# Sliding attention beside an FFT convolution on one core: offset pairs in partition groups, x by DMA transpose, 128-column FFT stationaries, two plane products, negative powers from conjugates

## The chip, the cores and the metric

The kernel runs on one core of one Trainium2 chip. The metric is the device time of one execution in microseconds (us), as a median over several runs. Engines are named as in the profile: PE is TensorE (matmuls), PEld its weight load, DVE is VectorE, ACT is ScalarE, POOL is GpSimd, and SP is SyncE, which here does nothing but issue DMA transfers. "L404" is a line of the kernel file.

## The reference, cut to what matters

Two independent halves are computed from different inputs and joined along the last axis.

```python
# A: 32 heads of 20 channels, 2048 positions; each position sees itself and
#    7 earlier ones, two apart
qkv    = x @ wqkv
logits = einsum("bhsd,bhswd->bhsw", q, k[pos - 2*w]) * scale     # w = 0..7, masked where < 0
o      = einsum("bhsw,bhswd->bhsd", softmax(logits), v[pos - 2*w]) @ wo
# B: a state-space convolution of 640 channels and 192 states, by FFT of length 4096
dt = exp(log_dt);  P = exp(dt * (A_re + 1j*A_im) * l)            # l = 0..2047
K  = einsum("dn,dnl,dn->dl", C, P, dt*B).real                    # the filter taps
y  = irfft(rfft(u) * rfft(K))[:2048] + u * Dskip
out = concat([A, B], axis=-1)                                    # 1 x 2048 x 1280, bf16
```

## The kernel before

Half B works in five chunks of 128 channels. For a chunk, DVE builds two tables of complex powers, X (20 coarse powers) and Y (33 fine powers), from a few generators that wait in DRAM. PE multiplies them into the filter taps ("kgen"). Then come two FFT steps (`f1`, `f2`), a complex product of spectra, and the first inverse step `ia`, whose result Z goes to DRAM for the second inverse step. Blocks of attention are put between the chunks. These are the parts that the argument below touches; cuts are marked with `...`.

```python
def table_tiles(pools):                       # two X tables, one Y table
    tp = pools["tab"]
    return (tp.tile([128, 20, 2, CW], bf16, name="Xtab", tag="Xtab", bufs=2), ...  # Xg
            tp.tile([128, NB, 2, CW], bf16, name="Ytab", tag="Ytab"))

def kgen(tc, pools, X, Y, Kd):
    ...                                       # matmuls of 20 x 33 into PSUM
        nc.scalar.copy(out=Kd[:, :, t0:t0 + nt], in_=ps[:].rearrange("p t b -> p b t"))

def f2_prod(tc, pools, C, A1, Yf):
    ...
            nc.scalar.copy(out=S[:, 2 * h:2 * h + 2], in_=ps[:])          # 512 elements in a row

def ia(tc, pools, C, Yf, Z):
    ...                                       # runs of 4 elements, 64 bytes apart
        nc.scalar.copy(out=Z[:, :, :, 4 * jq:4 * jq + 4].rearrange("p l r (j d) -> p (l r) j d", d=2),
                       in_=ps[:].rearrange("p j l r d -> p (l r) j d"))

    def make(c):                              # load generators, build tables, make the taps
            ...
            nc.sync.dma_start(out=XT[:, 0], in_=Gd[c, :, 12])
            nc.sync.dma_start(out=Xg[:], in_=Gd[c, :, 0:6])
            for k in range(6):
                nc.sync.dma_start(out=Y[:, 2 ** k], in_=Gd[c, :, 6 + k])
        X, Y = tables(tc, pools, tt[c])
        ...
        kgen(tc, pools, X, Y, Kds[c])
```

The softmax here doesn't subtract the row's maximum and nothing guards it: scores larger than these inputs give would overflow.

## Time and profile before

The time before is 511.86 us (median of 3 runs, 509.21 to 513.9).

| | before |
|---|---|
| span of the profiled run, mean granted clock | 511.0 us, 0.876 |
| busy: PE / DVE / ACT / POOL | 368.9 / 360.2 / 269.0 / 104.8 us |
| SP: DMA transfers issued, time spent issuing | 184, 93.7 us |
| DMA packets | 83,596 |

The first lines are from the page of the kernel before: its span, the busy time of every engine with share and number of instructions, and the shares of the chain of waits that ended last, by engine.

```profile
span 511.0 us, 13799 instructions
PE 368.9 (72%) x5943; PEld 243.2 (48%) x5943; DVE 360.2 (70%) x528; ACT 269.0 (53%) x517; POOL 104.8 (21%) x192
PE 36%; DVE 28%; DMA 15%; ACT 12%; issue 6%; SPq 1%; POOL 0%; ACTq 0%; POOLq 0%; DVEq 0%
```

No engine is full and the chain changes hands between PE and DVE. A table of windows tells more than an average. Its columns are the stretch, its length, and then for PE, PEld, DVE, ACT and POOL the busy time and the number of instructions, at last the granted clock, the DMA share and GB/s.

```profile
150.00:200.00 50.00, 30.35 (x765) 22.74 (x766) 46.51 (x68) 17.86 (x32) 2.36 (x9) 0.73 0.55 160
250.00:300.00 50.00, 39.84 (x703) 29.20 (x693) 48.05 (x62) 28.74 (x56) 11.66 (x22) 0.92 0.53 129
300.00:350.00 50.00, 42.56 (x837) 30.00 (x836) 44.13 (x62) 25.17 (x47) 11.64 (x22) 0.91 0.19 50
```

DVE is busy 44 to 48 of 50 us here: in the middle of the kernel DVE sets the pace. The ACT copies out of PSUM are these two groups, split by shape. The columns are line, engine, operation, out<-in, shapes, count, then busy us and mean ns of one, then the idle time before them and what ended it.

```profile
L365 ACT CAST Z<-ps_ia 128x512 bf16<-128x512 f32 x24 | 14.6, 676 | 9.1 <-PE ps_ia L364 9.0
L288 ACT CAST Kd<-ps_k 128x363 bf16<-128x363 f32 x10 | 4.6, 463 | 31.0 <-PE ps_k L286 31.0
```

The Z copies of 128x512 took 0.676 us on average, with their output in runs of 4 elements at 64-byte steps (alone in p1_probe, below, such runs took 585 ns, as contiguous output did). The prediction leaned on that 0.676.

### The profile page before, as it was taken

Reading aid. Unit: us, or ns where it says so; the run is one execution under the profiler, and the core shown is the slowest. Engines: PE = TensorE matmul, PEld = TensorE weight load, DVE = VectorE, ACT = ScalarE, POOL = GpSimd, SP = SyncE. Lnnn points to the kernel's source line nnn. Section 1 sums busy time; section 2 is a strip of 40 time slices with the busy share of each in tenths; the row PEclk is TensorE's granted clock in tenths of the full one; section 3 lists DMA queues with packets and bytes.
Section 4 is the critical chain, followed back from the end, with each engine's and each line's share of the span. In section 5 each row is a group of like instructions: output and inputs, shape, how many; then the busy total and the mean of one; then the engine's idle time right before and its main releaser. Section 6 shows DMA issues by size and latency. Waiting matters only on the chain.

```text
span 511.0 us, 13799 instructions
## 1 busy us (share of the span) xinstructions
PE 368.9 (72%) x5943; PEld 243.2 (48%) x5943; DVE 360.2 (70%) x528; ACT 269.0 (53%) x517; POOL 104.8 (21%) x192
## 2 busy tenths in 40 slices
PE   2868799874752778798879868699495855987720
PEld 1543334631220566666656755476263533765520
DVE  0326899651899997999999977998948753636012
ACT  4466895758682435656355723467224522656610
POOL 7605500055000001000170001070001341143012
PEclk9999999997795788799988978999779969997955
DMA  7964946359669352220236432043609597622262
GB/s 197 267 145 129 225 123 208 104 168 255 215 211 314 118 110 66 60 115 3 61 66 204 114 66 57 1 132 83 139 13 347 146 299 192 197 48 39 91 187 41
DMA packets 83596, 70.99 MB, mean 139 GB/s; under 512 B 51744, under 2 KB 75104, under 8 KB 81872
## 3 DMA queue, kind: packets, MB, share of 16 engines
q1 hardware_dynamic: 75456, 55.90, 39.0%
q0 software_dynamic: 6368, 13.16, 10.7%
q10 hardware_dynamic: 1712, 1.07, 0.8%
q8 instruction: 46, 0.75, 0.7%
q14 instruction: 14, 0.11, 0.1%
HBM read 42.86 MB, written 24.13 MB: 131 GB/s over the span
## 4 chain that ended last, share of the span: by engine, by line
PE 36%; DVE 28%; DMA 15%; ACT 12%; issue 6%; SPq 1%; POOL 0%; ACTq 0%; POOLq 0%; DVEq 0%
PE ps_o L493 6%; DVE krtmp L226 4%; PE ps_k L286 4%; PE ps_k L281 4%; PE ps_op L508 3%; DMA Gdram<-cs 3%; DMA xn<-in_A_x_dram 3%; PE ps_s L310 3%; ACT S L344 3%; DMA zq<-Zdram_61 3%; DMA out_dram<-ud 3%; DVE Ytab L225 3%; DVE prod L468 2%; PE ps_p L428 2%; DMA uq<-Udram 2%
## 5 line engine op out<-in xcount | busy, mean ns | idle before, releaser
L468 DVE TENSOR_TENSOR prod<-qb,kb 128x2048 bf16<-128x2048 bf16 x40 | 48.7, 1233 | 2.0 <-PE ps_l L471 2.0
L502 POOL DMA_DIRECT2D oT<-vb x64 | 36.7, 581 | 48.1 <-ACT vb L494 43.8
L429 ACT CAST st<-ps_p 128x512 bf16<-128x512 f32 x60 | 34.1, 581 | 12.6 <-PE ps_p L428 12.3
L428 PE MATMUL ps_p<-xT,w_324 128*128 128x512 bf16 x100 | 28.0, 439 | 13.7 <-ACT st L429 13.6
L364 PE MATMUL ps_ia<-cEA,Yf 128*32 128x256 bf16 x640 | 29.1, 333 | 7.9 <-DVE Yf L350 6.7
L494 ACT CAST vb<-ps_o 128x512 bf16<-128x512 f32 x20 | 13.1, 653 | 37.2 <-PE ps_o L493 37.1
L286 PE MATMUL ps_k<-Ytab,Xtab 64*20 64x33 bf16 x1280 | 25.8, 243 | 9.3 <-issue 9.2
L342 PEld LDWEIGHTS <-cT 128*64 128x64 bf16 x640 | 23.3, 114 | 18.9 <-issue 18.3
L288 ACT CAST Kd<-ps_k 128x363 bf16<-128x363 f32 (+1 forms) x15 | 6.8, 453 | 47.2 <-PE ps_k L286 47.2
L471 PE MATMUL ps_l<-prod,cGs 128*32 128x512 bf16 x160 | 18.3, 435 | 17.6 <-DVE prod L468 17.4
L225 DVE TENSOR_TENSOR Ytab<-Ytab 128x2688 bf16<-128x2688 bf16 (+3 forms) x25 | 30.8, 1234 | 0.0
L364 PEld LDWEIGHTS <-Yf 128*32 128x32 bf16 x640 | 23.3, 174 | 15.3 <-DVE Yf L350 8.2
L226 DVE TENSOR_TENSOR krtmp<-Ytab 128x2688 bf16<-128x2688 bf16 (+3 forms) x25 | 30.4, 1215 | 0.0
L281 PEld LDWEIGHTS <-Xtab 128*20 128x20 bf16 x1280 | 21.9, 125 | 14.9 <-issue 14.2
L493 PEld LDWEIGHTS <-cident 128*128 128x128 bf16 x160 | 14.9, 100 | 28.8 <-issue 14.4
L428 PE MATMUL ps_p<-xT,w_320 128*128 128x512 bf16 x100 | 25.6, 410 | 3.9 <-ACT st L429 2.8
L212 DVE TENSOR_TENSOR cs<-cs,am 128x768 bf16<-128x768 bf16 x22 | 12.2, 556 | 22.3 <-ACT cs L211 22.3
L292 POOL DMA_DIRECT2D Kd<-Kd x20 | 10.1, 514 | 86.6 <-ACT Kd L288 86.2
L286 PEld LDWEIGHTS <-Xtab 64*20 64x20 bf16 x1280 | 21.9, 121 | 12.2 <-issue 10.6
L244 POOL MEMSET Ytab<- 128x192 bf16 x5 | 1.4, 284 | 123.9 <-PE ps_k L286 123.9
L225 DVE TENSOR_TENSOR Xtab<-Xtab,Xg 128x768 bf16<-128x768 bf16 (+2 forms) x35 | 24.7, 706 | 2.2 <-DMA Xg<-Gdram 1.8
L281 PE MATMUL ps_k<-Ytab,Xtab 128*20 128x33 bf16 x1280 | 25.1, 246 | 1.1 <-DVE Ytab L229 0.5
(460 smaller groups left out, 948.7 us busy)
## 6 DMA issues: line engine op xcount, KB each, us to landing
HB<-k_HB SPq DMA_DIRECT2D x8, 1024.0 KB, 6.1
Gdram<-cs SPq DMA_DIRECT2D x24, 192.0 KB, 3.1
kb<-kd SPq DMA_DIRECT2D x4, 710.0 KB, 6.7
vb<-vd SPq DMA_DIRECT2D x4, 710.0 KB, 5.4
xn<-in_A_x_dram SPq DMA_DIRECT2D x8, 320.0 KB, 6.0
us<-in_B_u_dram POOLq DMA_DIRECT2D x16, 160.0 KB, 5.0
Udram<-uc POOLq DMA_DIRECT2D x8, 320.0 KB, 4.0
kd<-st SPq DMA_DIRECT2D x5, 512.0 KB, 5.8
```

Source lines behind the costliest of these rows:

```text
L225: V.tensor_tensor(out=full(O), in0=full(Y), in1=gb(gr), op=A.mult)
L226: V.tensor_tensor(out=full(t), in0=full(Y), in1=gb(gi), op=A.mult)
L281: MM(o, lhsT=X[:, :, part, col], rhs=Y[:, :, part, col], start=False, stop=False, tile_position=(0, 32 * g), skip_group_check=True)
L286: MM(o, lhsT=X[hb:hb + 64, :, part - 2, col], rhs=Y[hb:hb + 64, :, part - 2, col], start=False, stop=(part == 3), tile_position=(hb, 32 * ...
L342: nc.tensor.matmul(ps[64 * dd:64 * dd + 64, kk, r], lhsT=T[:, k, r, :], rhs=A1[:, k, :, 64 * dd:64 * dd + 64], start=(kk == 0 and r == 0), ...
L364: MM(o, lhsT=Yf[:, :, r, 4 * j + g], rhs=C["EA"][:, r, :], start=(jj == 0 and r == 0), stop=(r == 1), skip_group_check=True, tile_position ...
L428: nc.tensor.matmul(ps[:], lhsT=w[:, kt, 128 * ct:128 * ct + 128], rhs=self.xT[:, kt, 512 * sc:512 * sc + 512], start=(kt == 0), stop=(kt = ...
L429: nc.scalar.copy(out=st[:, sc], in_=ps[:])
L468: V.tensor_tensor(out=pr[:], in0=q[:, ct].unsqueeze(1).to_broadcast([128, 4, 4, 128]), in1=windows(k[:, ct, :, 8 - 8 * m:8 - 8 * m + 128], ...
L471: nc.tensor.matmul(ps[32 * sc:32 * sc + 32], lhsT=self.pools["Gs"][:, ct, :], rhs=pr[:, :, sc, :], start=(ct == 0), stop=(ct == 4), tile_p ...
L493: nc.tensor.matmul(ps[:], lhsT=self.ident[:], rhs=p2[:, w], start=(w == 0), stop=(w == W - 1))
L502: nc.gpsimd.dma_start(out=oT[32 * q:32 * q + 32, :, sc, :], in_=self.vb[qb][32 * sc:32 * sc + 32, q:DH:4, HALO:HALO + 128])
```

## The change

The intent was to take work from the busy engines. DVE loses the last doubling of Y (negative powers come from conjugates of the positive ones times a magnitude from ACT) and half of the spectrum product (two products of whole planes replace the four-part complex product). PE loses the transposes of x (a DMA transpose does them) and gets larger stationaries in the FFT steps. POOL loses the copies between attention and its projection, because the attention now puts two offsets in each of four partition groups. To fit, X has one buffer instead of two. The core of the diff, cut:

```diff
-            tp.tile([128, 20, 2, CW], bf16, name="Xtab", tag="Xtab", bufs=2)
+        self.X = tp.tile([128, 20, 2, CW], bf16, name="Xtab", tag="Xtab")            # one buffer
 # Y: 16 positive powers, then the negative ones
+            V.tensor_tensor(out=o, in0=Y[:, 17 + 8 * i:25 + 8 * i], in1=self.mg[i]..., op=A.mult)
+            V.tensor_scalar(out=neg, in0=neg, scalar1=-1.0, scalar2=None, op0=A.mult)
 # X[0] now also needs a value of Y
+        cmul(nc, X[:, 0:1], Xg[:, 6:7], self.Y[:, 32], tmp[:, 0:1], True)
 # taps
-        nc.scalar.copy(out=Kd[:, :, t0:t0 + nt], in_=ps[:].rearrange("p t b -> p b t"))
+            nc.scalar.copy(out=Kd[..., 8 * (q % 2):8 * (q % 2) + 8].rearrange("p b t -> p t b"), in_=ps[:])
 # spectrum: 128-column stationaries, k innermost in the output
-            nc.scalar.copy(out=S[:, 2 * h:2 * h + 2], in_=ps[:])
+            o = Sp[:, h, s0:s1, :, 4 * q:4 * q + 4].rearrange("p s t k -> p k (s t)")
+            nc.scalar.copy(out=o, in_=ps[h][:])
 # product: two products of planes
+        nc.vector.tensor_tensor(out=UT[:, h], in0=SK[:, h, 0], in1=UT[:, h], op=A.mult)
+        nc.vector.tensor_tensor(out=SK[:, h, 0], in0=SK[:, h, 0], in1=SU[:, h, 1], op=A.mult)
 # first inverse step
-        nc.scalar.copy(out=Z[:, :, :, 4 * jq:4 * jq + 4]..."p (l r) j d"..., in_=ps[:]...)
+            nc.scalar.copy(out=Z[:, :, 16 * h + 4 * tq:16 * h + 4 * tq + 4].rearrange("p x t -> p t x"), in_=ps[:])
 # transfers
+                nc.sync.dma_start_transpose(out=self.xT[...], in_=self.x[0][...])                       # 20
+                nc.sync.dma_start(out=v[t][32 * wg:32 * wg + 32], in_=self.vd[:, 4 * t:4 * t + 4, s0:s0 + PB + 2])  # 160
+                nc.sync.dma_start(out=U[32 * g:32 * g + 32, h], in_=usrc[g, c, :, h])                   # 40
```

## The prediction

> **What bounds the kernel now.** No engine is full: the page's busy table gives PE 369, DVE 360, ACT 269 of 511 us. In a table of windows DVE is busy 231 of the 250 us from 125 to 375: there it sets the pace. Outside it starves: 18 of the first 50 us, 16 of 90 to 125 (waiting for sines, which wait for its own shifts, and for the table's trip through DRAM), 58 of the last 136. The chain of waits agrees: DVE, PE and ACT alternate to 375 us; then come transfers (uq 8.4, zq 9.6 and 4.8, outputs 7.2 us) and a serial multiply, matmul, copy, add, store for each quarter of the inverse.
>
> **Costs**, by durations of the groups before. Single durations sum to 397 us on DVE for 360 busy, 299 on ACT for 269; I scale by 0.91 and 0.90.
>
> DVE loses
> - the last doubling of Y, 15 powers, 10.3 us a chunk: 51
> - half the spectrum product (0.69+0.69+0.44+0.42, x20, becomes 20 of 1.23): 20
> - the skip's add 6.6, reciprocals 3.8, the second shift.
>
> DVE gains
> - 16 negative powers: two multiplies of 3072 elements (1.75) and two sign flips a chunk: 22
> - absolute values for the cosine: 15 (estimate)
> - one more complex multiply in X: 6
>
> Attention's multiplies keep their elements. Sum 397 -> 346, busy about 315.
>
> ACT: x's copies (12) and quarter-turn activations (18.5) go; 80 exponentials (0.35, 28), Ln and Exp (6.5) and 16 more spectrum copies come. Sum 299 -> 312, busy about 280.
>
> PE: 5943 -> 5365 matmuls. The 80 transposes of x go, 640 inverse matmuls of 256 columns become 320 of 128, f1's 640 become 160, attention's sum uses four column groups. Busy 369 -> about 280.
>
> POOL loses the 64 oT copies (37 us), which stood between attention and projection; u -> Udram goes too. The price is 82k pieces of 32 bytes. The trace's 28-byte packets take 9 ns; over 16 engines that is an estimated 46 us, 9 a chunk, hidden by prefetch. This trace has no DMA transpose; [...] I allow 40.
>
> **On the critical path:** DVE's table and attention work, 125 to 375 us: about 45 us less. The start shortens by perhaps 20 (one shift, chunk 1 generated first). The tail loses oT's copies, the add after the inverse and Udram reads: about 35. The last chunk's chain stays: table, K, f1, f2, product, inverse, some 70 us of alternating PE and ACT.
>
> **Time:** 412 us, 8 in 10 within 375 to 458. Faster by over 2%: 0.94; within 2%: 0.04; slower: 0.02.
>
> **What would show it.** DVE busy 300 to 330; PE under 310; ACT 270 to 300; DVE at 85% or more from 60 to 320 us; Sp and Z copies at 0.6 to 0.7 us in spite of 64-byte write steps; no wait for U over 5 us.
>
> **What would make it wrong.** Transposes of x over 3 us each: ACT's first projection copy stands before its first sines, so the whole start slips. 421 transfers on SP's one queue (about 0.4 us an issue in the trace, 170 us in all) in an order in which one waits for another. Scattered ACT writes far slower than 0.65 us, making ACT the limit. Negative steps on DVE off the fast rate.

## The result, and the profile after

The changed kernel takes 679.3 us (median of 4 runs, 677.12 to 680.84), beside 512.88 us (509.21 to 515.29) for the kernel before on the same chip. The ratio is 1.3289, with a 95% interval of 1.3204 to 1.3375: a third slower, where 412 us had been predicted. A ratio here is the mean time of one kernel's fast runs over that of the other's fast runs of the same rounds, so it is not quite the ratio of the medians that are quoted. The result is correct.

From the page after: span, busy times, and the chain of waits by engine.

```profile
span 679.0 us, 12860 instructions
PE 387.0 (57%) x5356; PEld 235.1 (35%) x5364; DVE 310.2 (46%) x479; ACT 491.4 (72%) x601; POOL 36.3 (5%) x80
ACT 46%; PE 17%; SPq 11%; DMA 10%; DVE 10%; issue 5%; DVEq 0%; POOL 0%; ACTq 0%; POOLq 0%
```

DVE fell from 360 to 310 us and POOL from 105 to 36, as intended. ACT rose from 269 to 491 us, and the chain of waits, which ACT had held for 12%, is now ACT's for 46%. The groups of ACT's PSUM copies after, split by shape:

```profile
L404 ACT CAST Sp<-ps_f 128x512 bf16<-128x512 f32 x64 | 146.3, 2724 | 1.8 <-PE ps_f L400 1.8
L428 ACT CAST Z<-ps_ia 128x512 bf16<-128x512 f32 x40 | 92.0, 2743 | 8.9 <-PE ps_ia L427 8.8
L386 ACT CAST A<-ps_f 128x512 bf16<-128x512 f32 x80 | 42.0, 648 | 3.9 <-PE ps_f L385 3.8
L404 ACT CAST Sp<-ps_f 128x256 bf16<-128x256 f32 x32 | 37.5, 1546 | 2.4 <-PE ps_f L400 2.4
L349 ACT CAST Kd<-ps_k 128x264 bf16<-128x264 f32 x20 | 25.8, 1325 | 40.7 <-PE ps_k L347 40.7
```

Copies of the same 128x512 elements from PSUM take 0.65 us (A) or 2.72 us (Sp, Z). The three groups with single-element output steps take 301.6 us together (146.3 + 92.0 + 37.5 + 25.8). In windows after, ACT has taken DVE's place:

```profile
250.00:300.00 50.00, 27.10 (x659) 18.21 (x659) 16.14 (x19) 32.61 (x27) 1.55 (x5) 0.57 0.33 91
300.00:350.00 50.00, 24.49 (x236) 14.39 (x236) 30.18 (x45) 48.41 (x56) 1.05 (x2) 0.64 0.34 52
```

In the second row ACT is busy 48.4 of 50 us and DVE 30. Others wait for it; two lines of the waits (engine and line that waited, what it waited for, us in total, times, longest):

```profile
PE ps_f L400 <- ACT Sp L404: 70.1, 61, 3.4
DVE UT L414 <- ACT Sp L404: 48.1, 7, 14.7
```

Two more numbers differ from the prediction. The SP queue has 419 transfers that take 299.2 us to issue (before: 184 and 93.7 us); 160 of them, the V windows, take 89.6 us (0.56 us each) and the 40 loads of U, in pieces of 32 bytes, 57.2 us (1.43 us each, and up to 6.4). And the granted clock fell from 0.876 to 0.672.

### The profile page after: what moved, and what is told of

The parts are those of the page before. It is cut to its first block, busy times and chain, and to the rows that moved or that the text cites. A ratio compares the mean times of both kernels' runs of the same rounds, so it can differ in the third digit from the quotient of the medians.

```text
span 679.0 us, 12860 instructions
## 1 busy us (share of the span) xinstructions
PE 387.0 (57%) x5356; PEld 235.1 (35%) x5364; DVE 310.2 (46%) x479; ACT 491.4 (72%) x601; POOL 36.3 (5%) x80
## 4 chain that ended last, share of the span: by engine, by line
ACT 46%; PE 17%; SPq 11%; DMA 10%; DVE 10%; issue 5%; DVEq 0%; POOL 0%; ACTq 0%; POOLq 0%
ACT Sp L404 25%; ACT Z L428 11%; PE ps_p L463 3%; SPq L723 3%; PE ps_op L544 3%; SPq L445 3%; SPq L685 3%; DMA Gdram<-cs 2%; PE ps_k L347 2%; ACT mag L299 2%; PE ps_k L342 2%; ACT A L386 2%; DMA uq<-in_B_u_dram 1%; DVE p L529 1%; DMA Ytab<-Gdram 1%
## 5 line engine op out<-in xcount | busy, mean ns | idle before, releaser
L404 ACT CAST Sp<-ps_f 128x512 bf16<-128x512 f32 (+1 forms) x96 | 183.8, 2331 | 4.1 <-PE ps_f L400 4.1
L400 PE MATMUL ps_f<-A,cT 64*128 64x128 bf16 (+1 forms) x768 | 62.4, 263 | 73.5 <-ACT Sp L404 70.1
L428 ACT CAST Z<-ps_ia 128x512 bf16<-128x512 f32 x40 | 92.0, 2743 | 8.9 <-PE ps_ia L427 8.8
L463 PE MATMUL ps_p<-xT,w 128*128 128x512 bf16 x292 | 79.3, 418 | 21.0 <-ACT st L464 15.1
L529 DVE TENSOR_TENSOR p<-vb,attn 128x2048 bf16<-128x2048 bf16 x40 | 47.8, 1221 | 70.9 <-PE ps_o L532 48.6
L400 PEld LDWEIGHTS <-cT 64*128 64x128 bf16 x768 | 46.1, 120 | 97.2 <-issue 97.1
L349 ACT CAST Kd<-ps_k 128x264 bf16<-128x264 f32 x20 | 25.8, 1325 | 40.7 <-PE ps_k L347 40.7
L463 PEld LDWEIGHTS <-w 128*128 128x128 bf16 x300 | 30.5, 105 | 64.7 <-issue 36.1
L544 PE MATMUL ps_op<-wo,oT 128*128 128x320 bf16 x160 | 43.1, 423 | 16.2 <-ACT oT L535 15.8
L427 PE MATMUL ps_ia<-cE,Sp 128*128 128x128 bf16 x160 | 30.1, 274 | 32.5 <-ACT Z L428 21.3
L386 ACT CAST A<-ps_f 128x512 bf16<-128x512 f32 x80 | 42.0, 648 | 3.9 <-PE ps_f L385 3.8
L713 DVE TENSOR_TENSOR uq<-uq,Dsb 128x1536 bf16<-128x1536 bf16 (+1 forms) x8 | 6.6, 825 | 74.8 <-DMA uq<-in_B_u_dram 73.5
L427 PE MATMUL ps_ia<-cE,UT 128*128 128x128 bf16 x160 | 30.3, 275 | 0.0
```

Of the source, the lines that this page charges most:

```text
L386: nc.scalar.copy(out=A1[:].rearrange("p k r s t -> p (k r) s t")[:, :, sig, 8 * q:8 * q + 8], in_=ps[:])
L400: nc.tensor.matmul(ps[h][:, kk], lhsT=C["T"][hs, k, 64 * (1 - r):64 * (1 - r) + 128], rhs=A1[hs, k, r, s0:s1, :].rearrange("p s t -> p (s ...
L404: nc.scalar.copy(out=o, in_=ps[h][:])
L427: nc.tensor.matmul(ps[:, i], lhsT=X[:, h, 4 * t:4 * t + 4, :].rearrange("p g k -> p (g k)"), rhs=C["E"][:, n_, :], start=(i == 0 and n_ == ...
L428: nc.scalar.copy(out=Z[:, :, 16 * h + 4 * tq:16 * h + 4 * tq + 4].rearrange("p x t -> p t x"), in_=ps[:])
L463: nc.tensor.matmul(ps[:], lhsT=self.w[which][:, kt, 128 * ct:128 * ct + 128], rhs=self.xT[:, kt, 512 * sc:512 * sc + 512], start=(kt == 0) ...
```

## The experiments

My theory was that the cost of the scattered writes is the whole loss. The rivals were the long SP queue, the order that the scheduler chose, and the tail after the last product, and, later, a serial chain through the single X table. The runs are told in groups; each group ran on one chip beside the kernel before.

### Is it the scattered writes?

**e1_runs** exchanges the loops of the three copies. PSUM is now read with a long step and the output is written in runs of 4 elements (8 for Kd). The number and the order of instructions on every engine stay the same.

```diff
-            o = Sp[:, h, s0:s1, :, 4 * q:4 * q + 4].rearrange("p s t k -> p k (s t)")
-            nc.scalar.copy(out=o, in_=ps[h][:])
+            o = Sp[:, h, s0:s1, :, 4 * q:4 * q + 4].rearrange("p s t k -> p (s t) k")
+            nc.scalar.copy(out=o, in_=ps[h][:].rearrange("p k x -> p x k"))
 # and in the same way for Z (L428) and Kd (L349)
```

> The changed kernel with the loops of three ACT copies exchanged: Sp and Z are written in runs of 4 elements, Kd in runs of 8, and PSUM is read with the long step instead. Same values, and the same order of instructions on every engine. Theory S (an ACT write whose neighbours in time are 64 bytes apart costs about 5 ns an element): Sp of 512 falls from 2.72 to about 0.65 us, Z from 2.74 to 0.65, Kd from 1.33 to 0.45; ACT busy falls from 491 to about 240 us, and the span to 400-470. Rival D (the small DMA pieces on the SP queue, 32-byte loads of u and 516-byte loads of v, hold the loop): span stays above 600. Rival P (copies wait on PSUM traffic of PE, not on their own pattern): the copies stay above 2 us.

**e2_sp** does it for Sp alone.

> The changed kernel with only the Sp copy's loops exchanged; Z and Kd still scattered. Theory S: Sp 0.65 us, Z still 2.7, Kd still 1.3; ACT busy about 491-135-28=330 us; the span drops by most of the Sp share of the chain (168 us), to 510-560. Rivals D and P: above 600.

**e3_before_z2** goes the other way: in the kernel before, Z is written in runs of 2 elements (4 bytes) instead of 4, with the same 64-byte step.

```diff
-        nc.scalar.copy(out=Z[:, :, :, 4 * jq:4 * jq + 4].rearrange("p l r (j d) -> p (l r) j d", d=2), in_=ps[:].rearrange("p j l r d -> p (l r) j d"))
+        nc.scalar.copy(out=Z[:, :, :, 4 * jq:4 * jq + 4].rearrange("p l r (j d) -> p j (l r) d", d=2), in_=ps[:].rearrange("p j l r d -> p j (l r) d"))
```

> The other way round: the kernel before, its Z copy written in the order of PSUM, so in runs of 2 elements (4 bytes) at a 64-byte step instead of runs of 4. Theory S with a price per run (about 5 ns): 256 runs make the copy 1.3-1.5 us instead of 0.66, 40 copies cost ACT 30 us more. A price per element that is not in sequence would give the same 0.66. The span grows by 5-25 us, as ACT has slack there.

**p1_probe** runs the copy patterns alone, each four times in a row on one engine with nothing beside it. Its output is wrong, which doesn't matter for the time.

> No kernel of use, its output is zeros and so wrong on purpose: four ACT, four DVE copies of 512 elements of each pattern, alone on the chip. Theory S: ACT 0.6 us with a write step of 2 bytes, 2.7 us with 64 bytes; between them I expect a bend[...] (8-byte step still fast, 16 bytes and more slow). Runs of 2 at 64 bytes 1.3 us, of 4 and 8 0.6. Reading PSUM with a 512-byte step costs nothing. If the step of 64 bytes as such were at fault[...], 66 or 80 bytes would be fast. DVE writing with a 64-byte step: not known, expected slower than 0.69 us too.

Measured: e1_runs 534.77 us (532.13 to 535.62), 1.0472 of before (1.0419 to 1.0525). e2_sp 580.76 us (577.65 to 581.67), 1.1361 (1.1293 to 1.143). e3_before_z2 509.39 us, 0.9992 (0.9944 to 1.0039). The groups of e1_runs:

```profile
L404 ACT CAST Sp<-ps_f 128x512 bf16<-128x512 f32 x64 | 33.6, 618 | 7.4 <-PE ps_f L400 7.4
L428 ACT CAST Z<-ps_ia 128x512 bf16<-128x512 f32 x40 | 21.9, 592 | 25.1 <-PE ps_ia L427 25.1
L404 ACT CAST Sp<-ps_f 128x256 bf16<-128x256 f32 x32 | 10.4, 413 | 8.2 <-PE ps_f L400 8.2
L349 ACT CAST Kd<-ps_k 128x264 bf16<-128x264 f32 x20 | 7.6, 379 | 74.6 <-PE ps_k L347 74.6
```

The same copies take 73.5 us instead of 301.6, which is the whole fall of ACT's busy time (491.4 to 268.3 us). The time of the kernel falls by 144.5 us. In e2_sp the Sp copies have the fast times too (618 ns for 128x512, 417 for 128x256), but Z stays at 2740 ns and Kd at 1327 ns, and the kernel lies between the two. So the scattered writes are shown to be the cause of the step from 535 to 679 us. Both times missed the expected ranges, 400 to 470 for e1_runs and 510 to 560 for e2_sp: a second loss is left, since e1_runs is still 4.7% slower than before. e3_before_z2 had been expected 5 to 25 us slower and was the same; its Z copies, in runs of 2:

```profile
L365 ACT CAST Z<-ps_ia 128x512 bf16<-128x512 f32 x40 | 24.6, 684 | 13.2 <-PE ps_ia L364 13.0
```

What a pattern costs, by the durations of single instructions in the trace of p1_probe (512 elements on 128 partitions, ns, the median of four copies in a row):

| copy | output step or run | ns |
|---|---|---|
| ACT, PSUM to bf16 | contiguous (2 B) | 585 |
| | single elements, step 4 B | 726 |
| | step 8 B | 1290 |
| | step 16 B | 2419 |
| | step 32 B / 64 B / 66 B / 80 B / 128 B | 2292 / 2377 / 2372 / 2363 / 2434 |
| | runs of 2, of 4, of 8, each 64 B apart | 586, 585, 585 |
| | contiguous, PSUM read with a step of 512 B | 585 |
| ACT, PSUM to f32 | single elements, step 32 B | 1072 |
| ACT, SBUF to bf16 | contiguous, read contiguous / read at step 64 B | 617 / 1045 |
| DVE, PSUM to bf16 | contiguous / step 64 B / runs of 4 | 691 / 2377 / 692 |
| DVE, SBUF to bf16 | contiguous / written at step 64 B / read at step 64 B | 294 / 1280 / 592 |
| POOL, SBUF to bf16 (one copy each) | contiguous / step 64 B | 613 / 2402 |

Three things follow. A single bf16 element at a step of 16 to 128 bytes costs 3.4 to 4.4 times a contiguous one, on ACT (2292 to 2434 against 585 ns) and POOL (2402 against 613) as on DVE (2377 against 691 from PSUM, 1280 against 294 from SBUF; POOL and DVE at a step of 64 bytes): it is no quirk of ACT. Nothing ran on PE beside the copies (its two matmuls, 0.62 us each, were over before the first), so the price does not need traffic of PE in PSUM. Steps of 66 and 80 bytes are no better than 64 (2372 and 2363 against 2377 ns), so it is not the step of 64 bytes as such. And two neighbouring elements are enough to pay nothing (586 against 585 ns), which e3_before_z2 shows in the kernel too (Z at a mean of 684 ns). That refutes the first form of my theory, a price for each run. Nor did the bend come where I had expected it: the 8-byte step, expected to be fast, took 2.2 times as long as a contiguous copy (1290 against 585 ns), and even the 4-byte step cost 24% (726 ns). What in the hardware makes the price is not shown here; what is shown is that two neighbouring elements avoid it.

### What keeps e1_runs behind the kernel before?

The first ideas were the tail, the queue and the scheduler. All four runs start from e1_runs.

**x4_inv_early** puts the second inverse step of chunks 0 to 2 inside the loop, after the fourth chunk, where the kernel before has it.

```diff
+        if c == 3:
+            inverse([0, 1, 2], zsrc)
-    inverse([0, 1, 2], zsrc)
```

> On e1_runs (534.8 us): the inverse of chunks 0 to 2 is written into the loop after the attention of the fourth step, as in the kernel before, instead of after the loop. Theory T (the second loss is a tail in which all eight quarters of the inverse run alone, 63 us from 469 to 532, limited by transfers): about 20 to 30 us less, 505-515. Rival Q (the single SP queue, 309 us of issue, holds everything): under 10 us. Rival W (the order that the scheduler's timeline made holds the loop): under 10 us, as the earlier place is only a priority.

**x5_u_pool** issues the 40 loads of U from POOL instead of SP.

```diff
-                nc.sync.dma_start(out=U[32 * g:32 * g + 32, h], in_=usrc[g, c, :, h])
+                nc.gpsimd.dma_start(out=U[32 * g:32 * g + 32, h], in_=usrc[g, c, :, h])
```

> On e1_runs: the 40 loads of u in 32-byte pieces are issued by POOL instead of SP (same pieces, same bytes). Theory Q: SP's issue time falls by 60 us, the first loads of v no longer wait behind u (21 us of DVE's wait for vb), span 505-520. If the pieces themselves bind (81920 pieces on the 16 DMA engines): no change, or worse. The scheduler reorders the other engines too, so a few us either way are noise of the order.

**x7_all** has both, and issues the V windows, the skip inputs uq and half of the output stores from POOL as well.

```diff
-                nc.sync.dma_start(out=v[t]..., in_=self.vd...)
+                nc.gpsimd.dma_start(out=v[t]..., in_=self.vd...)
 # the same for U and uq; (nc.sync if g < 2 else nc.gpsimd) for the stores; early inverse of x4
```

> On e1_runs: the early inverse, and the loads of u, v, uq and half of the inverse's stores issued by POOL. Theories T and Q together: 460-490 us, SP issue time under 130 us. If W holds: above 510.

**x8_no_sim** takes away the block in which the compiler orders instructions by its own simulated timeline, so that they keep the order of the program.

```diff
-    ctx.enter_context(tc.block(name="body", schedule_with_timeline_sim=True))
```

> On e1_runs: one line removed, the block that lets a timeline model choose the order of instructions (part of the change); the order is then the default one, as in the kernel before. Theory W (the model does not know what copies and transfers cost, so its order is bad): 20-50 us less, 485-515. Rivals T and Q: within 10 us of e1_runs, or worse.

Measured: x4_inv_early 531.11 us, ratio to before 1.0369 (1.0285 to 1.0453). x5_u_pool 525.78 us, 1.0274 (1.0192 to 1.0355). x7_all 521.55 us, 1.0174 (1.0105 to 1.0242), with SP's issuing down to 121 us. x8_no_sim 546.09 us, 1.0642 (1.0554 to 1.073). All four missed what their theories expected: 505 to 515 for x4, 505 to 520 for x5, 460 to 490 for x7 and 485 to 515 for x8. The order of the scheduler is not the cause as supposed: in the order of the program the kernel is slower (other orders were not tried). e1_runs was not repeated beside these runs. Compared with its ratio of 1.0472 (1.0419 to 1.0525), the gain of x4 is within the noise, since the intervals overlap, and those of x5 and x7 are clear. So the queue has a part, and the tail perhaps a small one; even with both moves x7_all is still slower than before (by 1.1 to 2.4%).

### Is it the X table?

In windows, DVE of e1_runs is busy for only about 31 of every 50 us between 250 and 450 us, where the kernel before has 44 to 49 between 200 and 350 us. The same stretch of e1_runs as in the second row of the kernel before:

```profile
250.00:300.00 50.00, 30.42 (x630) 20.56 (x619) 31.48 (x48) 27.44 (x65) 2.61 (x6) 0.70 0.59 120
```

A new theory came from the buffers. With one X table, DVE can begin neither table of the next chunk while PE makes the taps from the present ones. With two, it builds the next X in that time.

**y1_before_x1** tests it in the kernel before, which has nothing else of the change.

```diff
-    return (tp.tile([128, 20, 2, CW], bf16, name="Xtab", tag="Xtab", bufs=2), ...
+    return (tp.tile([128, 20, 2, CW], bf16, name="Xtab", tag="Xtab", bufs=1), ...
```

> The kernel before with one buffer for the X table instead of two, which is the number that the changed kernel has; nothing else moves. Theory X (the remaining loss of e1_runs is a serial chain of tables on VectorE, then the generation of the kernel taps on TensorE, then the reload of the tables, because only one set of tables exists and the next X cannot be begun while the taps are made): the kernel before slows by 10 to 40 us. Rival (the loss sits elsewhere: DMA queue, first chunk, clock): within 5 us of before.

**d0_mem** is e1_runs with its memory cut so that a second X table will fit. It is the control for the next run.

```diff
-        return fp.tile([128, 2, 2, 64, 32], bf16, name="Sp", tag="Sp", bufs=2)
+        return fp.tile([128, 2, 64, 32], bf16, name="SU", tag="SU", bufs=2)     # and SK with one buffer
-            pr = p.tile([128, W, PB], bf16, name="prod", tag="prod", bufs=2)      # p2 likewise
+            pr = p.tile([128, W, PB], bf16, name="prod", tag="pp", bufs=3)        # shared with p2
 # V windows 5 buffers for 6, projections 2 for 3, start-up work tiles shared
```

> Control for d1_x2: e1_runs with its buffers made smaller so that a second X table will fit (the spectrum in two tiles, with 1 and 2 buffers, copied by twice as many ScalarE copies of half the size, products of the attention sharing 3 buffers, V windows with 5 buffers instead of 6). Both theories: 530 to 555 us, so 0 to 20 us worse than e1_runs (534.8).

**d1_x2** gives d0_mem the second X table, and frees X[0] of Y by a generator slot of its own. The two belong together, since a second table that still waits for Y could not be begun; "the second X table" stands for both below, and for the new order in which the tables are loaded and built. No run has only one of these.

```diff
-        self.X = tp.tile([128, 20, 2, CW], bf16, name="Xtab", tag="Xtab")
+        self.X = tp.tile([128, 20, 2, CW], bf16, name="Xtab", tag="Xtab", bufs=2)
-        cmul(nc, X[:, 0:1], Xg[:, 6:7], self.Y[:, 32], tmp[:, 0:1], True)
+        cmul(nc, X[:, 0:1], Xg[:, 6:7], self.Y[:, 32] if self.c == 0 else Xg[:, 7], tmp[:, 0:1], True)
 # Xg is loaded before Y's generators, and X is built before Y
```

> d0_mem with two buffers for the X table, X[0] made from a generator slot of its own instead of from Y, and X made before Y, so that VectorE can make the next X while TensorE makes the taps. Theory X: 20 to 50 us faster than d0_mem, VectorE idle less between the products. Rival: within 8 us of d0_mem.

**d2_best** is d1_x2 with all the moves of x7_all.

> d1_x2 and the helps of x7_all (inverse of the first three chunks after the fourth chunk's product, loads of U, V windows, skip input and half of the stores on the GpSimd queue). Theory X: 470 to 500 us, below the kernel before. Rival: 515 to 530 us, as x7_all (521.6).

Measured, one chip: before 509.5 us; y1_before_x1 535.44 us, ratio 1.0508 (1.0443 to 1.0573); d0_mem 532.94 us, 1.0467 (1.0398 to 1.0537); d1_x2 530.36 us, 1.0396 (1.0328 to 1.0463); d2_best 497.93 us, 0.9766 (0.9713 to 0.982).

In the kernel before, the second X table is worth 26 us (535.44 - 509.5). The mechanism can be read. In the kernel before, this is DVE in the time of chunk 1's taps, from its timeline (start us, duration, engine, line, operation, tiles, forms, count):

```profile
185.45 0.96 DVE L225 TENSOR_TENSOR Xtab<-Xtab,Xg 128x1536 bf16<-128x1536 bf16 x1
186.33 0.95 DVE L226 TENSOR_TENSOR krtmp<-Xtab,Xg 128x1536 bf16<-128x1536 bf16 x1
...
195.93 0.56 DVE L225 TENSOR_TENSOR Xtab<-Xtab,Xg 128x768 bf16<-128x768 bf16 x1
```

It builds the next X. In y1_before_x1 the load of that X can only be issued when the last matmul of the taps is over. The lines are from the timelines of PE, SP and DVE of y1_before_x1 (in brackets: idle time before, and what ended it):

```profile
182.07 1.86 PE L281 MATMUL ps_k<-Ytab,Xtab 128*20 128x33 bf16 x88
198.07 0.21 PE L286 MATMUL ps_k<-Ytab,Xtab 64*20 64x33 bf16 x1 [1.55 <-issue]
198.31 0.33 SPq L596 DMA_DIRECT2D Xtab<-Gdram  x1
201.93 0.36 DVE L225 TENSOR_TENSOR Xtab<-Xtab,Xg 128x384 bf16<-128x384 bf16 x1 [0.65 <-DMA Xtab<-Gdram]
```

The matmuls run from 182 to 198 us, the load follows 0.03 us after their end, and DVE's first multiply comes at 201.93. In the window from 150 to 200 us, DVE's busy time falls from 46.51 us to this:

```profile
150.00:200.00 50.00, 31.46 (x760) 23.38 (x761) 33.64 (x44) 18.70 (x34) 1.80 (x11) 0.71 0.51 148
```

So the theory holds for the kernel before. But d1_x2, which has the second table, is only 2.6 us faster than its control, and the intervals overlap; the expected 20 to 50 us did not come. d2_best is far better than either part. The timeline of d1_x2 tells why. First SP, then DVE:

```profile
212.48 3.45 SPq L688 DMA_DIRECT2D U<-in_B_u_dram  x2
216.04 10.79 SPq L496 DMA_DIRECT2D vb<-vd  x20
226.87 8.34 SPq L688 DMA_DIRECT2D U<-in_B_u_dram  x6
235.26 1.62 SPq L282 DMA_DIRECT2D Xg<-Gdram  x1
...
218.14 2.36 DVE L506 TENSOR_TENSOR prod<-qb,kb 128x2048 bf16<-128x2048 bf16 x2
242.12 0.36 DVE L261 TENSOR_TENSOR Xtab<-Xg 128x384 bf16<-128x384 bf16 x1 [21.62 <-DMA Xg<-Gdram]
```

The table is free, but its generators Xg stand in the one SP queue behind 20 loads of V windows and 8 loads of U, whose issuing takes 22.6 us. DVE stands still for 21.62 us until Xg has come. The wait for PE had become a wait for a transfer.

### Which of the three moves is needed with which?

Each of the next runs leaves one of the three moves out of d2_best: the early inverse, the POOL queues, the second X table. Their edits are those shown above.

> d2_best without the early inverse: d1_x2 with the loads of U, V windows, skip input and half of the stores on the GpSimd queue. Theory Q (in d1_x2 the loads of the next X generators stand behind the many small loads in the one SyncE queue, so that the second table only exchanges a wait for TensorE by a wait for that DMA): 500 to 510 us, most of d2_best's gain. Rival (the early inverse made the gain): 520 to 530 us.

> d2_best without the GpSimd queues: d1_x2 and the early inverse. Theory Q: 520 to 530 us, hardly faster than d1_x2 (530.4). Rival: 500 to 510 us.

> d2_best without the second X table: d0_mem with the GpSimd queues and the early inverse. Theory that the table and the queue are one chain, each useless alone: 515 to 525 us, as x7_all (521.6). Rival (the table has no part in it): 495 to 503 us, as d2_best.

Measured beside the kernel before at 511.57 us; the first, second and last rows are those above, so the ratios are the better comparison.

| run | 2nd X table | POOL queues | early inverse | us | ratio to before (95%) |
|---|---|---|---|---|---|
| d0_mem | | | | 532.94 | 1.0467 (1.0398 to 1.0537) |
| d1_x2 | yes | | | 530.36 | 1.0396 (1.0328 to 1.0463) |
| d5_x1_q_inv | | yes | yes | 527.41 | 1.0334 (1.0275 to 1.0393) |
| d4_x2_inv (*) | yes | | yes | 523.68 | 1.021 (1.0134 to 1.0286) |
| d3_x2_q | yes | yes | | 505.76 | 0.9899 (0.9849 to 0.995) |
| d2_best | yes | yes | yes | 497.93 | 0.9766 (0.9713 to 0.982) |

(*) One of the four runs of d4_x2_inv was slow (529.1 us). The ratio leaves it out; the median of the three fast ones is 523.13 us.

The second X table pays only together with the POOL queues. The table alone gains 0.7% of the time before (1.0467 to 1.0396, within the noise), the queues and the early inverse together without the table 1.3% (1.0467 to 1.0334), the table and the queues together 5.7% (1.0467 to 0.9899). Adding the queues to the table gives 5.0% without the early inverse and 4.4% with it; adding the table to the other two gives 5.7%. The queues alone, on d0_mem, were not run; and on e1_runs, with its larger buffers, the same queues and early inverse gained 3.0% (x7_all, 1.0472 to 1.0174), so they are not without worth by themselves, and the smaller buffers seem to take some of it. d3_x2_q came within its expected 500 to 510 us, d4 within 520 to 530; d5, at 527.41, was 2.4 us above its range. DVE's waits tell the same. The longest wait for the generators of X, from the waits of d4_x2_inv (table, no POOL queues) and then of d3_x2_q (both):

```profile
DVE Xtab L261 <- DMA Xg<-Gdram: 34.5, 3, 21.3
```

```profile
DVE Xtab L261 <- DMA Xg<-Gdram: 8.4, 2, 7.5
```

With both, it is 7.5 us instead of 21.3. In d5_x1_q_inv (POOL queues, one table) the trace has PE at the taps of chunks 1 to 3 from 152.3 to 175.5, from 247.8 to 270.2 and from 326.2 to 345.8 us. DVE's first multiply of the next table comes just after each of them, after a long idle time in brackets. From its timeline of DVE:

```profile
178.43 0.36 DVE L261 TENSOR_TENSOR Ytab<-Ytab 128x384 bf16<-128x384 bf16 x1 [27.37 <-DMA Ytab<-Gdram]
...
274.05 0.36 DVE L261 TENSOR_TENSOR Ytab<-Ytab 128x384 bf16<-128x384 bf16 x1 [25.55 <-PE ps_s L373]
...
348.86 0.36 DVE L261 TENSOR_TENSOR Ytab<-Ytab 128x384 bf16<-128x384 bf16 x1 [19.23 <-DMA Ytab<-Gdram]
```

DVE stands still while PE makes the taps, because the one table is in use and X[0] needs the Y that cannot be loaded yet. It is the same kind of wait that y1_before_x1 brought into the kernel before. d2_best beats both kernels, by 2.3% the one before (1.8 to 2.9%, so clear of equality) and by 27% the changed one (497.93 of 679.3 us). They were run at other times.

What stays open. Which of the transfers that moved to POOL are the ones that count was not tried with two tables; x5_u_pool moved U alone with one. And d2_best is still 86 us above the prediction. Its DVE is busy 309.1 of 496.0 us, so over a third of the span it is idle. The ends of the products of spectra in the two traces show where the 86 us lie (an estimate, since the prediction's stages do not end exactly there). The first chunk's product ends at 236 us, against 209 before: 27 us later, where the prediction had the start 20 us shorter. From there to the last product it takes 231 us, against 259 before: 28 less, where 45 had been predicted. After the last product, which ends at 467 us (469 before), the last inverse step takes until 496 us (511 before): 13 less, where 35 had been predicted. In the whole run DVE waits for the skip inputs uq for 44.3 us over six waits. So more than half of what is missing, 47 us, lies before the first product, and no experiment was aimed at it.

## Why the prediction was wrong

- **The step that failed** is "Sp and Z copies at 0.6 to 0.7 us in spite of 64-byte write steps". They took 2.72 and 2.74 us. I had taken the duration of the kernel before's Z copy, which also has a 64-byte step, and overlooked that it writes runs of 4 elements. ACT was predicted at 280 us busy and measured at 491.4; with the runs restored it measured 268.3. The prediction named "Scattered ACT writes far slower than 0.65 us, making ACT the limit" as a way to be wrong, and that is what came, but it gave no size and stood against a 0.94 chance of faster. The size is 228 us on ACT (301.6 - 73.5), of which 144.5 us were on the clock.
- **"DVE at 85% or more from 60 to 320 us" failed for another reason also.** Even without scattered writes DVE had 31.5 of 50 us from 250 to 300. The prediction took DVE's saved work for saved time, and did not see that the change from two X tables to one makes DVE wait for PE: 26 us in y1_before_x1, and 29 us between d5_x1_q_inv and d2_best (527.41 - 497.93). They were run at other times.
- **"The start shortens by perhaps 20"** failed too: in d2_best, with both losses mended, the first product still ends 27 us later than before. The cause of this stays open.
- **"421 transfers on SP's one queue (about 0.4 us an issue in the trace, 170 us in all)"** was mis-sized: 419 transfers took 299.2 us, 0.71 us each (299.2/419); in the kernel before the mean was already 0.51 (93.7/184). The count was right. The risk it named, an order in which one transfer waits for another, is what d1_x2 shows.
- **PE at 280 us** was measured at 387.0, and at 343.4 in e1_runs. The mean granted clock was 0.876 before, 0.672 after and 0.734 in e1_runs. I put a large part of the miss down to it, though no run varied it alone: busy time times mean clock gives 323 before (368.9 x 0.876), 260 after (387.0 x 0.672) and 252 in e1_runs (343.4 x 0.734). That is an estimate, as if all the busy time scaled with the mean clock; by it the work fell about as expected. What lowered the clock was not shown.
- **What was right.** DVE's sum: 315 us predicted, 310.2 measured, with the negative powers at 1.749 us for 3072 elements as costed. POOL fell from 104.8 to 36.3 us. The transposes of x did not slip: 20 issues of 1.26 to 2.5 us, 28.1 us in all, and the last of x had landed at 37.2 us, 32 us after the first issue at 5.2, where 40 were allowed. The 2.6 MB in 32 us are 82 GB/s. The pieces of 32 bytes took 8.9 ns each, where 9 was taken.
- **"No wait for U over 5 us"** held for the engines: the waits after name no engine that stood for U's transfer. But it looked in the wrong place. One U load took up to 6.4 us of SP's time to issue, and what waited was what stood behind it in the queue (in d1_x2 the generators Xg, behind 20 V windows and 8 U loads: DVE waited 21.62 us).

## What to carry to other kernels

When a layout change exchanges loops, look at the innermost output step of every copy, and not only at its largest step: here single bf16 elements 16 to 128 bytes apart cost four times a run of two (2292 to 2434 against 586 ns on ACT), while a read step of 512 bytes in PSUM cost nothing (585 ns, as contiguous; in SBUF a read step of 64 bytes did: 1045 against 617 ns on ACT), so the loops belong the other way round. When a rewrite gives up a second buffer, ask which engine worked in its shadow, and when it adds transfers to one queue, ask what stands behind them. Two such waits in a row can hide each other: here the second table alone showed nothing beyond the noise (1.0467 to 1.0396), so test such fixes together before calling either innocent.
